# Decay attention with a routed second attention: fixed key/query tiles with 64 extra rows, weights loaded later, and products of zeros on TensorE in the first three pairs

## The chip, the cores and the metric

The kernel runs on one core of one Trainium2 chip. The metric is the device time of one execution in microseconds (us). Lower is better.

## The reference, cut to what matters

```python
# q, k, v: (8, 8, 576, 64) f32; f: (8, 8, 576) in 0.8..1.0
scores = 0.125 * q @ k.T
cum = np.cumsum(np.log(np.clip(f, 1e-4, 1.0)), axis=-1)
scores = where(causal, -1e9, scores + cum[..., :, None] - cum[..., None, :])
x = softmax(scores) @ v                      # then heads side by side: (8, 576, 512)
logits = x @ w_gate                          # 4 experts, the best 2 kept per token
for e in range(4):                           # wq, wk, wv: (4, 512, 64); wo: (4, 64, 512)
    s = 0.125 * (x @ wq[e]) @ (x @ wk[e]).T  # causal
    out += gate[..., e:e+1] * (softmax(s) @ (x @ wv[e]) @ wo[e])
```

## The kernel before, in words

Work goes in *pairs*: two heads (or two experts) of one batch. Of each of the 8 batches there are 4 attention pairs (`a0` to `a3`) and 2 expert pairs (`m0`, `m1`), 48 in all. A pair passes through these stages.

- `prep_attn` (L202): keys and queries come in natural order (`kn`, `qn`), TensorE transposes them (L221), ScalarE copies the result, rounded, into the tile `kq` (L229) and VectorE writes the rest of the rounding into the tile `ka` (L230). Two transfers inside SBUF copy the rounded half into `ka` too (L199). `prep_moe` does the same for expert pairs by products with the weights.
- `extra_rows` (L187): rows 64 to 68 of `kq` carry the decay. On the key and the query side they hold a cumulated logarithm in two parts, and ones or minus ones against it, so that one product gives score plus decay. For the first two pairs (`DIRECT = 2`) they are written by POOL memsets (L189, L190) and by two transfers from the tile `chl` (L191, L192). For all later pairs one transfer brings 5 rows from the DRAM buffer `ex` (L194). Row 68 takes the row maximum.
- `max_pass` (L369): products of `kq` with itself over 68 rows (L378), each reduced by VectorE to row maxima (L384, L395). TensorE turns the maxima (L433), ScalarE negates them (`ms`, L435), and two transfers put them into row 68 of `kq` (L199).
- `scores` (L454): the products of `ka` (L464) and of `kq` over 69 rows (L465), exponentials on ScalarE (L481 to L512), causal masks and partial row sums on POOL. `attend` (L537) multiplies by the values (`oa`, `ob`, L551).

`decay_rows` (L117) makes `chl` for all heads at the start, laid out as 32 rows of two heads, and fills `ex` with the ones, the minus ones and `chl` (L139 to L144). `load_weights` (L150) loads, splits and rounds wv, wk, wq and wo in 8 pieces of up to 576 columns: transfers (L164 to L174), a ScalarE copy (L175), a POOL subtraction (L176).

Each stage is a generator. A table gives it a start and an end on a scale on which one pair is 1.0 (`PLAN`, `HEAD` for the first 9 pairs, `TAIL` for the last), and a heap emits the pieces in that order. The weights have `l0=-1.0` to `l1=0.2` in the table `W`. A scheduler then sets the final order on each engine by priority and its own timeline. All transfers are issued by one queue, SP, in order. Each engine also runs its list in order.

```python
    def extra_rows(kq, x):
        if x < DIRECT:
            nc.gpsimd.memset(kq[64:69].bitcast(F32), 1.0)
...
        nc.sync.dma_start(
            kq[64:69].bitcast(F32), ex[x].rearrange("k r h s -> r h k s")
        )
```

Of the kernel before, what the change touches and what calls it, by code (L numbers as in the profile page):

```python
# [23 lines left out]

@with_exitstack
def tile_decay_attention_moe(ctx: ExitStack, tc, q, k, v, f, w_gate, wq, wk, wv, wo, out):
# [83 lines left out]
    ft, lf = (fl[:NP, i, : 2 * S] for i in range(2))  # L112
    nc.sync.dma_start(ft, f.rearrange("b (p h) s -> (b p) (h s)", h=2))
    chl = pair.tile([128, 2, 2, S], F32R, tag="kq", name="chl")[:NX]
    nc.gpsimd.memset(chl[NP:].bitcast(F32), 0.0)
# [654 lines left out]
```

## Time and profile before

| | |
|---|---|
| runs of the kernel | 794.36, 796.29, 798.07 us (median 796.29) |
| the profiled execution | 794.9 us, its span 793.2 us |
| mean granted TensorE clock | 0.994 |
| busy over the span: TensorE / weight load | 93% / 76% |
| busy: VectorE / ScalarE / POOL | 73% / 60% / 51% |
| DMA | 73.32 MB, mean 92 GB/s |
| chain that ended last | TensorE 74%, VectorE 8%, ScalarE 6%, DMA 5% |

In 40 equal slices of the span TensorE is busy 3, 6, 9, 8 tenths in the first four, 9 in nearly all others, and 8, 9, 9, 8, 7 in the last five. The DMA engines are busy 7, 8, 6, 5 tenths in the first four slices and about 3 later. The first 53.4 us are called the head below: they end with the last product of the first pair's `ob`.

### The profile page before, as it was taken

The page shows a single profiled execution, that of the slowest core. Times are in us where ns is not written, and L with a number is a line of the kernel's source. Part 1 is how long each engine was busy: PE and PEld are TensorE (multiplying, and loading weights), DVE is VectorE, ACT ScalarE, POOL GpSimd, SP SyncE. Part 2 cuts the span into 40 slices and gives each one's busy share as a digit, 9 for nine tenths or more (in the row PEclk, how much of TensorE's full clock was granted, in tenths as well). Part 3 has the DMA queues.
Part 4 walks back from the last instruction along what each step waited for, and adds up shares of the span by engine and source line. Part 5 has one row for each costly group of instructions (what it writes and reads, how often), then busy time and mean ns, then how long its engine had stood idle before and what let it go on. Part 6 is the DMA issues. An engine that isn't in the chain of part 4 may idle for free.

```text
span 793.2 us, 16781 instructions
## 1 busy us (share of the span) xinstructions
PE 740.0 (93%) x5704; PEld 600.7 (76%) x5704; DVE 581.6 (73%) x1858; ACT 472.8 (60%) x1152; POOL 400.8 (51%) x763
## 2 busy tenths in 40 slices
PE   3698999998999999999999999999999999989987
PEld 2475678776897788877887778878887768869854
DVE  7557786898777797787777787778777877764633
ACT  5465664575657674676556665667655755555443
POOL 7556472556446564547444644465544564473270
PEclk9998999999999999999999999999999999999999
DMA  7865541254424632355323542256323442203103
GB/s 187 194 138 118 98 105 32 58 123 89 91 51 105 145 86 49 84 128 139 79 63 87 127 107 63 52 135 147 78 65 79 112 102 57 55 21 70 58 14 106
DMA packets 143231, 73.32 MB, mean 92 GB/s; under 512 B 124085, under 2 KB 124565, under 8 KB 143081
## 3 DMA queue, kind: packets, MB, share of 16 engines
q1 hardware_dynamic: 143147, 72.26, 39.9%
q8 instruction: 45, 0.74, 0.4%
q14 instruction: 39, 0.32, 0.1%
HBM read 32.68 MB, written 10.96 MB: 55 GB/s over the span
## 4 chain that ended last, share of the span: by engine, by line
PE 74%; DVE 8%; ACT 6%; DMA 5%; SPq 3%; issue 2%; POOL 2%; POOLq 0%; ACTq 0%; DVEq 0%
PE pp_m L352 13%; PE ob_a L551 9%; PE pv L276 6%; PE po L678 6%; PE s_a L464 6%; PE s_a L465 6%; PE m_a L378 5%; PE tp_a L221 3%; PE ob_m L551 3%; PE m_m L378 3%; PE s_m L464 3%; PE s_m L465 3%; PE oa_a L551 2%; DVE junk_a L384 2%; PE sm_a L594 2%
## 5 line engine op out<-in xcount | busy, mean ns | idle before, releaser
L230 DVE TENSOR_TENSOR ka_a<-tp_a,kq_a 64x288 fp32r<-64x288 f32 x256 | 113.0, 451 | 25.0 <-ACT kq_a L229 19.4
L384 DVE CUSTOM_DVE_ANT_0 junk_a<-m_a,mask 128x192 bf16<-128x192 f32 (+2 forms) x192 | 93.3, 486 | 48.2 <-PE m_a L378 28.6
L464 PE MATMUL s_a<-ka_a 128*128 128x320 f32 (+4 forms) x384 | 115.8, 319 | 1.7 <-ACT P_a L481 1.1
L378 PE MATMUL m_a<-kq_a 68*128 68x320 f32 (+4 forms) x384 | 103.5, 337 | 14.0 <-DMA kq_a<-chl 7.8
L229 ACT ACTIVATE kq_a<-tp_a 64x288 fp32r<-64x288 f32 x256 | 99.1, 403 | 28.7 <-DVE ka_a L230 18.8
L465 PE MATMUL s_a<-kq_a 69*128 69x320 f32 (+4 forms) x384 | 104.8, 302 | 3.1 <-DMA kq_a<-ms_a 3.1
L450 POOL TENSOR_SCALAR_AFFINE_SELECT P_a<-P_a 128x128 f32<-128x128 f32 x128 | 37.5, 295 | 107.5 <-ACT P_a L496 96.1
L483 POOL TENSOR_SCALAR_AFFINE_SELECT P_a<-P_a 128x256 f32<-128x256 f32 x64 | 26.1, 408 | 125.8 <-ACT P_a L481 124.1
L378 PEld LDWEIGHTS m_a<-kq_a 68*128 68x128 f32 (+1 forms) x384 | 65.5, 191 | 26.4 <-issue 9.1
L359 ACT ACTIVATE kq_m<-pp_m 64x288 fp32r<-64x288 f32 x128 | 51.5, 405 | 51.4 <-PE pp_m L352 29.9
L360 DVE TENSOR_TENSOR ka_m<-pp_m,kq_m 64x288 fp32r<-64x288 f32 x128 | 57.8, 454 | 31.6 <-ACT kq_m L359 27.0
L464 PEld LDWEIGHTS s_a<-ka_a 128*128 128x128 f32 (+1 forms) x384 | 71.1, 186 | 8.8 <-ACT P_a L496 2.2
L519 POOL TENSOR_TENSOR R_a<-P_a 128x448 f32<-128x448 f32 x64 | 73.2, 1144 | 4.1
L551 PE MATMUL ob_a<-P_a,va 128*64 128x320 f32 (+1 forms) x512 | 73.8, 433 | 0.9 <-ACT ms_m L435 0.4
L465 PEld LDWEIGHTS s_a<-kq_a 69*128 69x128 f32 (+1 forms) x384 | 70.1, 186 | 5.7 <-DMA kq_a<-ms_a 4.3
L551 PEld LDWEIGHTS ob_a<-P_a,va 128*64 128x64 f32 x512 | 36.0, 144 | 33.4 <-issue 8.0
L464 PE MATMUL s_m<-ka_m 128*128 128x192 f32 (+3 forms) x192 | 57.9, 316 | 1.9 <-ACT P_m L496 1.2
L384 DVE CUSTOM_DVE_ANT_0 junk_m<-m_m,mask 128x192 bf16<-128x192 f32 (+2 forms) x96 | 46.6, 485 | 17.7 <-PE m_m L378 14.1
L520 POOL TENSOR_TENSOR R_a<-R_a,P_a 128x320 f32<-128x320 f32 x64 | 55.9, 875 | 1.1
L465 PE MATMUL s_m<-kq_m 69*128 69x192 f32 (+2 forms) x192 | 52.5, 300 | 3.3 <-DMA kq_m<-ms_m 3.2
L378 PE MATMUL m_m<-kq_m 68*128 68x192 f32 (+2 forms) x192 | 48.0, 317 | 0.6 <-DVE mxt_m L395 0.3
L276 PE MATMUL pv<-vh,xh_a 128*128 128x260 f32 x160 | 47.1, 294 | 1.1 <-DVE ka_a L230 1.0
(189 smaller groups left out, 2071.8 us busy)
## 6 DMA issues: line engine op xcount, KB each, us to landing
ka_a<-kq_a SPq DMA_DIRECT2D x64, 288.0 KB
kn_a<-in_k_dram SPq DMA_DIRECT2D x64, 144.0 KB
qn_a<-in_q_dram SPq DMA_DIRECT2D x64, 144.0 KB
ka_m<-kq_m SPq DMA_DIRECT2D x32, 288.0 KB
va<-in_v_dram SPq DMA_DIRECT2D x64, 128.0 KB
out_dram<-outb SPq DMA_DIRECT2D x32, 256.0 KB
kq_a<-ex SPq DMA_DIRECT2D x30, 45.0 KB
kq_a<-ms_a SPq DMA_DIRECT2D x64, 2.5 KB
```

The lines of the kernel that those rows point to most:

```text
L229: nc.scalar.activation(hv, src, AF.Copy)
L230: nc.vector.tensor_tensor(lo[:, h, gs], src, hv.bitcast(F32), ALU.subtract)
L276: nc.tensor.matmul(pv[:, :NV], l[c][:, t0 : t0 + 128], r[:, c], start=(n == 0), stop=(n == 3 * KC - 1))
L352: nc.tensor.matmul(pp[:, :HS], w[:, c, es], x[c][:, gs], start=(n == 0), stop=(n == 3 * KC - 1))
L360: nc.vector.tensor_tensor(lo[:, h, gs], src, hv.bitcast(F32), ALU.subtract)
L378: nc.tensor.matmul(dst, qB[0:K, h, i0 : i0 + dst.shape[0]], kB[0:K, h, j0:j1], start=True, stop=True)
L384: nc.vector.tensor_tensor_reduce(jk[:, :n], src, mask[:, MW - n :], 1.0, init, ALU.add, ALU.max, acc)
L464: nc.tensor.matmul(dst, kaf[:, c : c + m], qA[:, h, i0:i1], start=True, stop=False)
L465: nc.tensor.matmul(dst, kqf[0:K, c + h * S : c + h * S + m], qB[0:K, h, i0:i1], start=False, stop=True)
L519: g.tensor_tensor(r[:, h, 128:S], q[:, 320:768], q[:, 768:1216], ALU.add)
L520: g.tensor_tensor(r[:, h, 256:S], r[:, h, 256:S], q[:, 1216:1536], ALU.add)
L551: mm = nc.tensor.matmul(dst[64 * h : 64 * h + 64, c0 : c0 + rhs.shape[-1]], vs[h][0:kp, blk], rhs, start=first, stop=last,)
```

## The change

- **Key/query tiles.** `kq` no longer comes from a pool of three buffers that holds `chl` too. Four fixed tiles `kq0` to `kq3` are taken in turn. Rows 64 to 127 of each are set once (`constant_rows`: ones on the key side, zeros on the query side, minus ones in query rows 64 and 65), the first tile partly by VectorE, the rest by POOL. `max_pass` and `scores` now multiply over all 128 rows (`K = 128`). The natural tiles get four buffers in place of three.
- **Decay rows.** `decay_rows` works on 64 rows of one head each. `ex` holds only the two parts of the logarithm, in one transfer (L180), and zeros for the expert pairs. Per pair two transfers (L242, L243) of 2 rows each replace the one of 5 rows. Only the first pair takes its rows from `chl` (`DIRECT = 1`).
- **Weights.** They are due from 1.0 to 4.0 on the plan's scale, in 9 pieces: two experts in one transfer (L217).
- **Products of zeros.** `warm` multiplies a tile of zeros, 128 x 128 by 128 x 512 in BF16, into a PSUM tile that nobody reads: 8 at the start, and one behind each ScalarE copy of the first three pairs, 24 in all, each waiting for that copy.
- `PLAN`, `HEAD` and `TAIL` are moved and keep their numbers. `dynamic_dma_scratch_size=1024` frees SBUF. The asserts emit nothing.

```diff
+WARM = (1, 1, 1)
+WARM0 = 8
+W = dict(d1=-1.9, l0=1.0, l1=4.0, c0=-1.7, c1=-1.3, x0=-0.9)
...
-    nat = ctx.enter_context(tc.tile_pool(name="nat", bufs=3))
+    nat = ctx.enter_context(tc.tile_pool(name="nat", bufs=4))
...
+    NKQ = 4
+    kqs = [const.tile([128, 2, 2, S], F32R, name=f"kq{i}") for i in range(NKQ)]
+    wz = const.tile([128, 512], BF16, name="wz")
+    nc.vector.memset(wz, 0.0)
+    wps = ptile(ps_o, "o", "warm")
+    def warm(n, after=None):
+        for _ in range(n):
+            mm = nc.tensor.matmul(wps, wz[:, 0:128], wz, start=True, stop=True)
+            if after is not None:
+                together(mm, after)
+    def constant_rows(kq, eng):
+        eng.memset(kq[64:128, :, 0].bitcast(F32), 1.0)
+        nc.gpsimd.memset(kq[64:128, :, 1].bitcast(F32), 0.0)
+        nc.gpsimd.memset(kq[64:66, :, 1].bitcast(F32), -1.0)
+    constant_rows(kqs[0], nc.vector)
...
-    DIRECT = 2
-    ex = dram.tile([NX, 2, 5, 2, S], F32, name="ex")
+    DIRECT = 1
+    ex = dram.tile([NP + 1, 2, 2, S], F32, name="ex")
...
-        for kq, r0, r1, src in ((0, 2, 5, pos1), (1, 0, 2, neg1), (1, 4, 5, pos1)):
-            nc.sync.dma_start(
-                ex[:, kq, r0:r1].rearrange("x r h s -> x (r h) s"),
-                src.unsqueeze(1).to_broadcast([NX, 2 * (r1 - r0), S]),
-            )
-        nc.sync.dma_start(ex[:, 0, 0:2], chl.bitcast(F32))
-        nc.sync.dma_start(ex[:, 1, 2:4], chl.bitcast(F32))
+    def spread_rows():
+        nc.sync.dma_start(ex[:NP].rearrange("x h r s -> (x h) r s"), chl.bitcast(F32))
+        nc.sync.dma_start(
+            ex[NP].rearrange("h r s -> (h r s)").rearrange("(p c) -> p c", p=128), zero
+        )
...
+                for e in range(0, E, 2):
+                    parts.append(
+                        (w[e : e + 2].rearrange("e (c p) d -> p (e c) d", p=128), 2, slice(D * e, D * e + 2 * D))
+                    )
+                if nm == "v":
+                    parts.append((w_gate.rearrange("(c p) e -> p c e", p=128), 1, slice(E * D, NV)))
...
-        nc.sync.dma_start(
-            kq[64:69].bitcast(F32), ex[x].rearrange("k r h s -> r h k s")
-        )
+        src = ex[x].rearrange("h r s -> r h s")
+        nc.sync.dma_start(kq[64:66, :, 0].bitcast(F32), src)
+        nc.sync.dma_start(kq[66:68, :, 1].bitcast(F32), src)
...
-                    nc.scalar.activation(hv, src, AF.Copy)
+                    made = nc.scalar.activation(hv, src, AF.Copy)
                     nc.vector.tensor_tensor(lo[:, h, gs], src, hv.bitcast(F32), ALU.subtract)
+                    if u["first"] is not None:
+                        warm(WARM[u["first"]], made)
...
-        kB, qB, K = u["kB"], u["qB"], 68
+        kB, qB, K = u["kB"], u["qB"], 128
...
-        qA, qB, K = u["qA"], u["qB"], 69
+        qA, qB, K = u["qA"], u["qB"], 128
...
-    W = dict(d1=-0.8, l0=-1.0, l1=0.2)
...
-    task(-1.99, W["d1"], 1.0, decay_rows)
+    task(-1.999, W["d1"], 1.0, decay_rows)
+    task(W["c0"], W["c1"], 1.0, constants)
+    task(W["x0"], W["x0"], 1.0, spread_rows)
     task(W["l0"], W["l1"], 4.0, load_weights)
```

What it does to the order is shown at three places. First SP, from the second half of the second pair's copies to the row maxima (`ms`) of the first pair, before:

```order
L169 DMA st_q_353<-in_moe_wq_dram 128x4x64 [waits DMAHW1_49]
L169 DMA st_q_353<-in_moe_wq_dram 128x4x64 [waits DMAHW2_49]
L199 DMA ka_a_1_254<-kq_a_1_255 64x2x576 [waits DMAHW3_49,Activation_49]
L191 DMA kq_a_1_255<-chl 2x2x576 [waits DMAHW4_49,Pool_49]
L192 DMA kq_a_1_255<-chl 2x2x576 [waits DMAHW5_49]
L164 DMA st_o_365<-in_moe_wo_dram 128x512 [waits DMAHW6_49,Pool_49]
L211 DMA kn_a_2_389<-in_k_dram 96x6x64 [waits DMAHW7_49,PE_49]
L211 DMA kn_a_2_389<-in_k_dram 96x6x64 [waits DMAHW0_49]
L211 DMA qn_a_2_390<-in_q_dram 96x6x64 [waits DMAHW1_49,PE_49]
L211 DMA qn_a_2_390<-in_q_dram 96x6x64 [waits DMAHW2_49]
L199 DMA kq_a_0_163<-ms_a_0_305 1x5x128 [waits DMAHW3_49,Activation_49]
L199 DMA kq_a_0_163<-ms_a_0_305 1x5x128 [waits DMAHW4_49]
```

and now:

```order
L259 DMA qn_a_3_512<-in_q_dram 96x6x64 [waits DMAHW0_49]
L299 DMA va_104<-in_v_dram 128x4x64 [waits DMAHW1_49]
L299 DMA va_104<-in_v_dram 128x4x64 [waits DMAHW2_49]
L304 DMA va_104<-in_v_dram 64x2x64 [waits DMAHW3_49]
L299 DMA va_105<-in_v_dram 128x4x64 [waits DMAHW4_49]
L246 DMA ka_a_2_372<-kq_113 64x2x576 [waits DMAHW5_49,Activation_49]
L299 DMA va_105<-in_v_dram 128x4x64 [waits DMAHW6_49]
L304 DMA va_105<-in_v_dram 64x2x64 [waits DMAHW7_49]
L246 DMA kq_111<-ms_a_0_316 1x5x128 [waits DMAHW0_49,Activation_49]
L246 DMA kq_111<-ms_a_0_316 1x5x128 [waits DMAHW1_49,PE_49]
L217 DMA st_v_619<-in_moe_wv_dram 128x8x64 [waits DMAHW2_49]
L217 DMA st_v_672<-in_moe_w_gate_dram 128x4x4 [waits DMAHW3_49]
```

Ahead of the row maxima the weights are gone but for one piece of wv, and the loads of the fourth pair and of the first values stand there now.

Second ScalarE, from the row maxima of the first pair (`ms_a_0`) to its first exponentials (`P_a_0`), before:

```order
L435 ACTIVATE ms_a_0_305<-mp_a_0_303 10x128 [waits PE_49]
L175 ACTIVATE qh<-st_q_340 128x512 [waits DMAHW7_49,DMAHW0_49]
L175 ACTIVATE qh<-st_q_353 128x512 [waits DMAHW2_49,DMAHW1_49]
L175 ACTIVATE oh<-st_o_365 128x512 [waits DMAHW6_49]
L229 ACTIVATE kq_a_2_388<-tp_a_2_395 64x288 [waits DMAHW4_49,PE_49,DMAHW5_49,Activation_49,Pool_49]
L229 ACTIVATE kq_a_2_388<-tp_a_2_444 64x288 [waits PE_49]
L229 ACTIVATE kq_a_2_388<-tp_a_2_395 64x288 [waits DVE_49]
L175 ACTIVATE oh<-st_o_409 128x512 [waits DMAHW5_49]
L229 ACTIVATE kq_a_2_388<-tp_a_2_444 64x288 [waits DVE_49]
L481 ACT_TABLE_LOAD
L481 ACTIVATE P_a_0_369<-s_a_0_371 128x512 [waits PE_49]
```

and now:

```order
L489 ACTIVATE ms_a_0_316<-mp_a_0_314 10x128 [waits PE_49]
L277 ACTIVATE kq_114<-tp_a_3_629 64x288 [waits PE_49]
L538 ACT_TABLE_LOAD [waits PE_49]
L538 ACTIVATE P_a_0_354<-s_a_0_356 128x512 [waits Activation_49]
L220 ACTIVATE vh<-st_v_619 128x4x128 [waits DMAHW2_49]
L220 ACTIVATE vh<-st_v_672 128x4x4 [waits DMAHW3_49]
L538 ACTIVATE P_a_0_354<-s_a_0_406 128x512 [waits PE_49]
```

No weight stands between the row maxima and the first exponentials any more. Four pieces stand among the exponentials of the first pair and the rest behind them.

Third TensorE, in the second pair's maximum pass (`m_a_1`), before:

```order
L378 MATMUL m_a_1_381<-kq_a_1_255 128x192
L378 MATMUL m_a_1_381<-kq_a_1_255 128x320
L378 MATMUL m_a_1_403<-kq_a_1_255 128x192
L378 MATMUL m_a_1_403<-kq_a_1_255 128x320
L378 MATMUL m_a_1_413<-kq_a_1_255 128x256
L378 MATMUL m_a_1_420<-kq_a_1_255 128x448
L221 MATMUL tp_a_2_395<-ident,kn_a_2_389 128x96 x3
L221 MATMUL tp_a_2_444<-ident,kn_a_2_389 128x96 x3
L378 MATMUL m_a_1_413<-kq_a_1_255 128x256
L221 MATMUL tp_a_2_474<-ident,qn_a_2_390 128x96 x2
L465 MATMUL s_a_0_371<-kq_a_0_163 128x192
```

and now:

```order
L432 MATMUL m_a_1_395<-kq_112 128x256 [waits DVE_49]
L432 MATMUL m_a_1_402<-kq_112 128x448 [waits DVE_49]
L432 MATMUL m_a_1_395<-kq_112 128x256 [waits DVE_49]
L432 MATMUL m_a_1_413<-kq_112 128x448 [waits DVE_49]
L432 MATMUL m_a_1_417<-kq_112 128x320 [waits DVE_49]
L432 MATMUL m_a_1_417<-kq_112 66x64 x2
L432 MATMUL m_a_1_436<-kq_112 128x320 [waits DVE_49]
L519 MATMUL s_a_0_356<-kq_111 128x192 [waits DMAHW0_49]
```

The first scores that need the row maxima (`s_a_0<-kq`) stood inside the second pair's maximum pass, and stand behind all of it now. The 24 later products of zeros all stand ahead of the second pair's maximum pass.

## Rows read from the trace of the kernel before

**Rows 1.** Busy us of PE, PEld, DVE, ACT, POOL; clock; DMA share; GB/s.

```profile
0.00:53.40 53.40, 31.55 (x131) 23.26 (x131) 32.31 (x88) 26.48 (x57) 32.38 (x61) 1.00 0.79 179
31.20:53.40 22.20, 20.60 (x92) 15.94 (x92) 13.31 (x42) 12.04 (x28) 10.73 (x18) 1.00 0.78 167
53.40:107.00 53.60, 48.00 (x339) 33.94 (x339) 41.85 (x128) 32.60 (x82) 31.12 (x60) 0.90 0.51 105
200.00:740.00 540.00, 526.76 (x4208) 438.10 (x4210) 408.35 (x1332) 333.35 (x819) 273.42 (x523) 1.00 0.38 87
```

**Rows 2.** Timeline of TensorE, head: start us, length us, instruction [idle before <-releaser].

```profile
18.93 1.30 PE L378 MATMUL m_a<-kq_a 68*128 68x192 f32 x4 [3.04 <-DMA kq_a<-chl]
31.19 1.30 PE L378 MATMUL m_a<-kq_a 68*128 68x192 f32 x4 [4.72 <-DMA kq_a<-chl]
35.53 0.51 PE L465 MATMUL s_a<-kq_a 69*128 69x192 f32 x1
49.88 3.44 PE L551 MATMUL ob_a<-P_a,va 128*64 128x320 f32 x16
```

**Rows 3.** Timeline of TensorE: the same two shapes early and late.

```profile
46.25 0.47 PE L465 MATMUL s_a<-kq_a 69*128 69x320 f32 x1
57.44 0.31 PE L465 MATMUL s_a<-kq_a 69*128 69x320 f32 x1
47.04 1.55 PE L551 MATMUL oa_a<-P_a,va 128*64 128x256 f32 x8
59.53 0.87 PE L551 MATMUL oa_a<-P_a,va 128*64 128x256 f32 x8
```

**Rows 4.** Timeline of SP's queue, head.

```profile
3.38 2.02 SPq L139 DMA_DIRECT2D ex<-one  x3
24.54 2.31 SPq L169 DMA_DIRECT2D st_q<-in_moe_wq_dram  x4
32.06 1.55 SPq L199 DMA_DIRECT2D kq_a<-ms_a  x2
```

**Rows 5.** Timeline of ScalarE, head.

```profile
37.18 0.63 ACT L175 ACTIVATE oh<-st_o 128x512 fp32r<-128x512 f32 x1 [0.92 <-DMA st_o<-in_moe_wo_dram]
38.12 1.28 ACT L481 ACT_TABLE_LOAD   x1
39.42 1.08 ACT L481 ACTIVATE P_a<-s_a 128x512 f32<-128x512 f32 x2
47.48 0.26 ACT L512 ACTIVATE pl<-s_a 64x128 f32<-64x128 f32 x1
```

**Rows 6.** Timeline of VectorE, head.

```profile
16.36 1.38 DVE L230 TENSOR_TENSOR ka_a<-tp_a,kq_a 64x288 fp32r<-64x288 f32 x3 [0.23 <-ACT kq_a L229]
19.78 0.36 DVE L384 CUSTOM_DVE_ANT_0 junk_a<-m_a,mask 128x192 bf16<-128x192 f32 x1 [2.04 <-PE m_a L378]
25.66 0.28 DVE L428 TENSOR_REDUCE mxs_a<-mx_a 64x2 f32<-64x128 f32 x1
```

**Rows 7.** Group by line, ScalarE, 18 to 40 us: busy us, mean ns.

```profile
L175 ACT ACTIVATE kh<-st_k 128x512 fp32r<-128x512 f32 x2 | 1.3, 631 | 3.1 <-DMA st_k<-in_moe_wk_dram 3.1
```

**Rows 8.** Groups by line, POOL, 0 to 60 us.

```profile
L176 POOL TENSOR_TENSOR kl<-st_k,kh 128x512 fp32r<-128x512 f32 x2 | 2.5, 1261 | 1.2 <-DMA st_q<-in_moe_wq_dram 1.0
L190 POOL MEMSET kq_a<- 2x1152 f32 x2 | 2.1, 1054 | 0.1
```

**Rows 9.** Waits, 107 to 740 us: us in total, times, longest us.

```profile
PEld s_m L465 <- DMA kq_m<-ms_m: 4.7, 6, 1.4
PEld s_a L465 <- DMA kq_a<-ms_a: 4.3, 5, 1.3
PE s_m L465 <- DMA kq_m<-ms_m: 3.2, 4, 1.1
PE s_a L465 <- DMA kq_a<-ms_a: 3.1, 5, 1.1
```

**Rows 10.** Tile kq_a, 107 to 740 us: duration ns min/median/max.

```profile
L194 SPq DMA_DIRECT2D kq_a<-ex x24: 742/768/904, 153.0 to 648.3; - x24
```

More of the change, by code (lines that the diff above doesn't have):

```diff
@@ L106, in tile_decay_attention_moe @@
     NP = B * NPH
-    NX = NP + 1
-    DIRECT = 2
-    ex = dram.tile([NX, 2, 5, 2, S], F32, name="ex")
+    DIRECT = 1
+    ex = dram.tile([NP + 1, 2, 2, S], F32, name="ex")
+    NR = B * H
     fl = prob.tile([128, 2, 1536], F32, tag="P", name="fl")
[L112 to L115, printed above, removed]
@@ new lines, in tile_decay_attention_moe @@
+    ft, lf = (fl[:NR, i, :S] for i in range(2))
+    nc.sync.dma_start(ft, f.rearrange("b h s -> (b h) s"))
+    chl = rows.tile([128, 2, S], F32R, tag="R", name="chl")[:NR]
+    pos1 = rows.tile([128, 2, S], F32, tag="R", name="one")[:NR, 0]
+    nc.vector.memset(pos1, 1.0)
+    zero = const.tile([128, 4 * S // 128], F32, name="zero")
+    nc.vector.memset(zero, 0.0)
+    warm(WARM0)
+    def decay_rows():
+        cum = prob.tile([128, 2, 1536], F32, tag="P", name="cum")[:NR, 0, :S]
+        nc.scalar.activation(lf[:, 0:1], pos1[:, 0:1], AF.Ln)
+        nc.vector.tensor_scalar(ft, ft, 1.0e-4, 1.0, ALU.max, ALU.min)
+        nc.scalar.activation(lf, ft, AF.Ln)
+        nc.vector.tensor_tensor_scan(cum, pos1, lf, 0.0, ALU.mult, ALU.add)
+        nc.scalar.activation(chl[:, 0], cum, AF.Copy, scale=INV_SCALE)
+        nc.vector.scalar_tensor_tensor(
+            chl[:, 1], cum, INV_SCALE, chl[:, 0].bitcast(F32), ALU.mult, ALU.subtract
+        )
+        yield 1.0
@@ new lines, in load_weights @@
+            for i, (src, ne, at) in enumerate(parts):
+                st = xs.tile([128, S], F32, tag="xh", name=f"st_{nm}{i}")
+                if ne is None:
+                    nc.sync.dma_start(st[:, :DM], src)
+                    sv = st[:, :DM]
+                    h, l = hi[:, at[0]], lo[:, at[0]]
+                else:
+                    k = ne * n * (at.stop - at.start) // ne
+                    nc.sync.dma_start(st[:, :k].rearrange("p (x d) -> p x d", x=ne * n), src)
+                    sv = st[:, :k].rearrange("p (e c d) -> p c e d", e=ne, c=n)
+                    h, l = (t[:, :, at].rearrange("p c (e d) -> p c e d", e=ne) for t in (hi, lo))
+                nc.scalar.activation(h, sv, AF.Copy)
+                nc.gpsimd.tensor_tensor(l, sv, h.bitcast(F32), ALU.subtract)
+                yield 4.0 / 9
@@ L185, in new_pair @@
+    def new_pair(u, nm):
+        ka = pair.tile([128, 2, 2, S], F32R, tag="ka", name="ka" + nm)
+        i = n_pair[0] % NKQ
+        n_pair[0] += 1
+        assert kq_user[i] is None or kq_user[i].get("scored")
+        kq_user[i] = u
+        kq = kqs[i]
         return ka, ka[:, 0], ka[:, 1], kq, kq[:, :, 0], kq[:, :, 1]
@@ L261, in moe_front @@
             vm = [v_att[0], v_att[1]]
+            assert all(u is None or u.get("attended") for u in v_user[:2]) and natt[0] == B * NPH
         else:
@@ L710, in tile_decay_attention_moe @@
     for i, (kind, b, p) in enumerate(seq):
-        u = dict(kind=kind, b=b, p=p)
+        u = dict(kind=kind, b=b, p=p, first=i if i < len(WARM) else None)
         t = pos[i]
```

164 lines of the change are left out of this document (70 added, 94 removed).

## The prediction, as put on record

> **What bounds the kernel now.** I read the busy times by stretch first, to see where TensorE is not at work, then the timelines of the head, engine by engine, and last the waits of the long middle. From 200 to 740 us TensorE is busy 526.8 of 540 us [rows 1]: there TensorE is the bound, and a head that ends earlier moves everything behind it forward by as much. In the head, the first 53.4 us, TensorE is busy 31.6 us and the DMA engines carry 179 GB/s at a share of 0.79, against 0.38 later [rows 1]. What to see there are three things.
>
> Transfers come late. The first pair's maximum pass starts at 18.93 us and had waited for the decay rows (`kq_a<-chl`); the second pair's starts at 31.19, after 4.72 us of waiting for the same kind of rows [rows 2]. SP issues one transfer behind the other, among them ones and minus ones for `ex` at 3.38 us and weights at 24.54, and comes to the row maxima only at 32.06 [rows 4].
>
> ScalarE then waits for weights. It runs in order, and a piece of wo at 37.18 us that had waited for its transfer, and a table load at 38.12, stand ahead of the first exponentials, which run at 39.42 [rows 5]. The scores they read had begun at 35.53 [rows 2].
>
> TensorE is slow. The granted clock reads 1.00 in the head [rows 1], but the same product of 320 columns takes 0.47 us at 46.25 and 0.31 at 57.44, and the eight of `oa` take 1.55 us and then 0.87 [rows 3]. So before some 53 us it runs at the lower of its two levels, 1.2 GHz, and behind it at 2.4. By the column of the clock alone, products of zeros have nothing to gain, and only the sum below is left (787.5); by the durations, a case of 782 stands beside it (the first rival). The Trainium skill (TensorE: Matmul & The Clock Gate, Part 1) says that the half rate is the default and that activity lifts it, and warns that clock events in a trace can't be fully trusted. The durations agree with it.
>
> **The change part by part.** The sum goes along the first pair, up to the end of its `ob`, which is at 49.88 + 3.44 us and four small products, about 53.4 [rows 2].
>
> *Transfers ahead of the first decay rows.* By their shapes, f, four loads of keys and four of queries, the ones (33 x 12 x 576 x 4 bytes, 912 KB), `chl` into `ex` twice (608 KB), a piece of wv and half a copy make 3.27 MB before. Now it is f, the same eight loads, two for the third pair, a larger piece of wv and the half copy: 2.19 MB. The difference at 179 GB/s [rows 1] is 6.1 us, so the rows should land at about 13 us in place of 18.9.
>
> *VectorE is late next.* Before, the last splits of the second pair end at 16.36 + 1.38 = 17.7 us [rows 6]. The work on the logarithms halves, since 64 rows go at once, and memsets of about 1.4 us come in, so I put this 1 to 2 us earlier, and the maximum pass of the first pair, which now stands ahead of the last of these splits, at 15.5. The pass takes 19.78 to 25.94, 6.2 us [rows 6], and stands mixed with 9 splits of 0.46 us (three take 1.38 [rows 6]), so it ends at about 26. That is no gain. But the second pair's pass follows at once, because its rows are there, and ends at about 32, where before it began at 31.19 [rows 2] and ended far behind the first scores.
>
> *The scores.* They now stand behind that pass, and begin at about 32 in place of 35.53. This loses part of what the earlier rows give. `ms` has until then: about 37 transfers stand ahead of it, at about 0.7 us each (two for 1.55 [rows 4]) some 26 us, so it is issued at about 27 and hidden by the second pass.
>
> *The exponentials.* No weight stands ahead; one us of products and the table load of 1.28 us [rows 5] do. They start at about 34.2 in place of 39.42: 5.2 us gained. From there to the end of the last exponential (`pl`, 47.74 [rows 5]) it was 8.3 us; that stretch holds 4.3 us of exponentials and copies and now 2.4 us of weights and small pieces, 6.7 in all: 1.6 us gained. Behind it TensorE has `oa`, `ob`, transposes and the end of the third pair's pass, 6.3 us at the low clock, against 5.7 before: 0.6 us lost. The end of `ob` comes at about 47.2, **6.2 us earlier**.
>
> *What is done by then.* The third pair's maximum pass is done, of which before two thirds, 4 us on VectorE, were still to come; fewer splits of the fourth pair are done. The next stretch has TensorE busy 48.0 and VectorE 41.9 of 53.6 us [rows 1], so work ahead is worth something but not its full length: between 0 and 4 us, I take **2**, nearer the one us that TensorE needs for it.
>
> *The weights* leave the head. A piece costs ScalarE 0.63 us [rows 7] and POOL 1.26 us [rows 8]. Five of nine come behind the first exponentials, 3 us on ScalarE and 6 on POOL, where these are busy 32.6 and 31.1 of 53.6 us [rows 1]. That idle time hides them, and without this cover it would be up to 3 us on the path. I take **0.3** lost.
>
> *The products of zeros.* No row shows one. By the 0.31 and 0.47 us for 320 columns [rows 3], 512 columns take at most 0.50 or 0.75 us. The 24 behind copies take 12 to 18 us on TensorE, which in the first 31.2 us is busy only 31.6 - 20.6 = 11 us [rows 1]: they fit in its idle time. But each waits for a ScalarE copy, and transposes and maximum products queue behind it. The bounds are 0 and, one behind every second of fourteen products, 4 us; VectorE is the slower one there and has two PSUM tiles to read, so I take **0.4** lost. For the clock I take nothing in the sum: the last of them stands ahead of the second pair's pass, and that pass is limited by VectorE, so TensorE has little to do from about 26 to 32 us and I expect it at the low level when the scores begin.
>
> *Constant rows.* Eleven memsets of 1152 elements on POOL at 1.05 us [rows 8], 11.6 us, replace about 8 us of memsets; POOL has nothing else early. Products over 128 rows in place of 68 or 69: `ka` with 128 rows and `kq` with 69 take turns in the chain, and the time goes by columns; at nothing, with no bound beyond 0.
>
> *The long middle.* Of `ex`, 94 transfers of two rows replace 46 of five (two for 47 pairs, one for 46), each at about 0.77 us of SP [rows 10], and bytes fall from 45 to 18 KB a pair. SP is idle in between, so nothing; the bounds are in the rivals. A fourth buffer for `nat` may give a us. The scheduler shuffles the order everywhere, plus or minus 2 us.
>
> Sum: 6.2 + 2 - 0.3 - 0.4 = **7.5 us** off the profiled 794.9: 787.4, called 787.5. The median of the runs shown is 796.29, 1.4 above that execution, so a like median could be 789. A measurement of this kernel tells about 0.5%, 4 us, from no change: faster means under 792.3.
>
> **The rivals.**
>
> *The clock stays up.* If the zeros lift TensorE to 2.4 GHz and it holds through the first scores, `oa` and `ob` lose 0.7 and 1.3 us ([rows 3], and `ob` in proportion), the products ahead of the exponentials about 1.5: 784. From 53.4 to 107 the mean clock is 0.90 [rows 1], which is about 5 us lost; if the earlier state also keeps some of this, 779 to 784, I say 782. For it: TensorE at the low level is busy 20.6 of 22.2 us just before 53.4 [rows 1], so there it does set the pace. Against: the idle stretch of the second pass.
>
> *The gain is given back.* The weights meet value loads and natural tiles at 40 to 80 us, where DMA carries 105 GB/s already [rows 1]; ScalarE stops in order behind each late piece, and the exponentials with it. Two stops like the 0.9 us at 37.18 [rows 5] for each of four pairs, 7 us: no change, 792.5 to 797.
>
> *More transfers, slower.* Place: SP, just ahead of the row maxima of a pair. In the middle the first scores wait for them 4.7 + 4.3 + 3.2 + 3.1 = 15.3 us in 20 waits [rows 9]. If the extra issue of 0.77 us [rows 10] falls between `ms` being ready and its issue, the wait grows by it. With 10 such pairs of 47 the gain is gone; with all 20 that wait now and the 4 us on both sides of a late landing it is 15 us lost: 802. Against it: one transfer of 45 KB becomes two of 9 KB, and an issue stands directly ahead of `ms` in only few pairs. The Trainium skill (DMA: Bandwidth & Descriptors, Bandwidth) says that transfers under 64 KB are dominated by their descriptors and should be merged, which speaks against the split; no row here shows the smaller size.
>
> **How the numbers follow.** Forecast (low clock, 787.5, from 783.5 to 791.5 by the bounds of the terms): 0.50. The clock stays up (782): 0.26. Given back (792.5 to 797): 0.16. More transfers (802): 0.08. The first two are faster: 0.76; same 0.16; slower 0.08. The range goes from 779, the low end of the second, to 794.5, the middle of the third, and leaves out 0.08 above it by the last, about 0.08 of the third, and a little below.
>
> **What would show it.** Right: the first pair's maximum pass at 15 to 16 us, the second's directly behind, first exponentials near 34, the end of `ob` near 47, and products of 320 columns at 0.47 us between 32 and 45. If those take 0.31, it is the second case. Wrong: a head that ends at 50 or later, pauses of ScalarE before weights from 35 to 70 us, or longer waits for `ms` in the middle than 15 us.

## The result, and the profile after

The changed kernel takes 787.2 us in the median (785.06 to 788.92, 6 runs) against 795.3 (792.63 to 798.61, 6 runs) for the kernel before on the same chip. The ratio is 0.9896, with an interval from 0.9862 to 0.9929: **faster by about 1%**. The profiled execution takes 786.67 us with a span of 785.0.

TensorE bounds the middle, so I read first where its span goes: busy or idle. Busy times by engine, from the page of the kernel before:

```profile
span 793.2 us, 16781 instructions
PE 740.0 (93%) x5704; PEld 600.7 (76%) x5704; DVE 581.6 (73%) x1858; ACT 472.8 (60%) x1152; POOL 400.8 (51%) x763
```

The same part of the page after:

```profile
span 785.0 us, 16899 instructions
PE 740.4 (94%) x5735; PEld 594.7 (76%) x5736; DVE 584.9 (75%) x1857; ACT 469.5 (60%) x1151; POOL 404.0 (51%) x770
```

The products of zeros alone, of the changed kernel, 0 to 60 us (busy us of PE; clock; DMA share; GB/s):

```profile
0.00:60.00 60.00, 13.07 (x31) 0.86 0.91 173
```

Before, TensorE is idle for 793.2 - 740.0 = 53.2 us, after for 785.0 - 740.4 = 44.6. Its busy time is the same only by chance: 13.1 us of it are zeros (the trace has 31 of the 32), so the real products take 727.3 us, 12.7 less than before. So the 8.2 us are 8.6 us less idle time; 12.7 us of faster products were paid back by 13.1 us of zeros.

Busy times by stretch, after (columns as in [rows 1]):

```profile
0.00:53.40 53.40, 43.35 (x220) 28.13 (x222) 38.63 (x115) 29.71 (x71) 35.01 (x74) 0.84 0.93 174
31.20:53.40 22.20, 19.72 (x122) 14.69 (x123) 14.72 (x54) 15.51 (x38) 16.85 (x29) 0.91 0.92 170
53.40:107.00 53.60, 46.30 (x337) 35.05 (x338) 46.96 (x120) 34.67 (x83) 33.36 (x60) 0.94 0.51 111
200.00:740.00 540.00, 525.67 (x4217) 434.71 (x4216) 410.23 (x1335) 329.97 (x816) 272.71 (x520) 1.00 0.36 85
```

From 200 to 740 us nothing has changed against [rows 1]. In the head VectorE does 38.6 us of work where it did 32.3, and from 53.4 to 107 it is busy 47.0 us in place of 41.9. The timeline of TensorE, head, after:

```profile
16.04 0.50 PE L432 MATMUL m_a<-kq 128*128 128x192 f32 x2
...
27.37 1.30 PE L432 MATMUL m_a<-kq 128*128 128x192 f32 x4
...
33.29 0.36 PE L519 MATMUL s_a<-kq 128*128 128x192 f32 x1
...
34.52 0.47 PE L519 MATMUL s_a<-kq 128*128 128x320 f32 x1
...
39.19 0.30 PE L519 MATMUL s_a<-kq 128*128 128x320 f32 x1
...
42.96 0.87 PE L600 MATMUL oa_a<-P_a,va 128*64 128x256 f32 x8
...
44.76 2.16 PE L600 MATMUL ob_a<-P_a,va 128*64 128x320 f32 x16
...
46.75 0.28 PE L600 MATMUL ob_a<-pl,va 128*64 128x64 f32 x4
```

The first pass begins at 16.04 us, the second follows at 27.37 without the wait of 4.72 us of [rows 2], and the first `ob` ends at 47.03 in place of 53.4. The 320 columns take 0.47 us at 34.52 and 0.30 at 39.19, so the clock rises in the middle of the first pair's scores and not at 53 us [rows 3]. VectorE between the two passes:

```profile
26.65 0.28 DVE L482 TENSOR_REDUCE mxs_a<-mx_a 64x2 f32<-64x128 f32 x1
28.23 0.36 DVE L438 CUSTOM_DVE_ANT_0 junk_a<-m_a,mask 128x192 bf16<-128x192 f32 x1 [1.30 <-PE m_a L432]
...
34.12 0.28 DVE L482 TENSOR_REDUCE mxs_a<-mx_a 64x2 f32<-64x128 f32 x1
```

ScalarE at the first exponentials:

```profile
34.32 1.28 ACT L538 ACT_TABLE_LOAD   x1 [4.73 <-PE s_a L519]
35.61 0.60 ACT L538 ACTIVATE P_a<-s_a 128x512 f32<-128x512 f32 x1
36.11 0.72 ACT L220 ACTIVATE vh<-st_v 128x512 fp32r<-128x512 f32 x2
...
41.33 0.26 ACT L569 ACTIVATE pl<-s_a 64x128 f32<-64x128 f32 x1
```

No weight stands ahead of them now, and the weights behind them (`vh`) had landed in time: none of the waits of ScalarE from 35 to 70 us is for a weight. The transfers of SP that matter:

```profile
9.10 0.80 SPq L238 DMA_DIRECT2D kq<-chl  x1
...
30.11 1.65 SPq L246 DMA_DIRECT2D kq<-ms_a  x2
```

The waits for row maxima from 107 to 740 us, which were 15.3 us in 20 waits [rows 9], are 11.9 in 22:

```profile
PEld s_m L519 <- DMA kq<-ms_m: 5.4, 10, 0.9
...
PEld s_a L519 <- DMA kq<-ms_a: 3.4, 5, 1.2
PE s_m L519 <- DMA kq<-ms_m: 3.1, 7, 0.7
```

The lead of 6.4 us at the first `ob` grows to 15.7 at the fourth (94.0 before, 78.3 after), falls to 5.4 at the ninth (170.5 and 165.1), and is 8.1 at the last. TensorE's clock has a part in these swings. Behind the head it falls to 0.50 twice more in either kernel, each time behind a stretch in which TensorE had paused: before from about 73 to 80 and from 90 to 93.5 us, after from 97 to 103 and from 161.5 to 165, some 10 us in each. In the changed kernel, around the first of these falls, and from the first `ob` to the ninth (busy us of PE; clock; DMA share; GB/s):

```profile
93.50:96.50 3.00, 1.29 (x11) 1.00 0.97 205
97.00:103.00 6.00, 5.93 (x26) 0.50 0.03 6
47.03:165.10 118.07, 107.73 (x840) 0.96 0.43 95
```

### The profile page after: what moved, and what is told of

It reads as the page before. It is cut to its first block, busy times and chain, and to the rows that moved or that the text cites. A ratio compares the mean times of both kernels' runs of the same rounds, so it can differ in the third digit from the quotient of the medians.

```text
span 785.0 us, 16899 instructions
## 1 busy us (share of the span) xinstructions
PE 740.4 (94%) x5735; PEld 594.7 (76%) x5736; DVE 584.9 (75%) x1857; ACT 469.5 (60%) x1151; POOL 404.0 (51%) x770
## 4 chain that ended last, share of the span: by engine, by line
PE 74%; DVE 10%; ACT 6%; DMA 5%; issue 2%; SPq 2%; POOL 1%; POOLq 0%; DVEq 0%; ACTq 0%
PE pp_m L406 13%; PE ob_a L600 8%; PE pv L330 7%; PE po L727 7%; PE s_a L518 6%; PE m_a L432 6%; PE s_a L519 5%; PE tp_a L269 4%; PE s_m L519 3%; PE m_m L432 3%; PE s_m L518 3%; DMA kq<-ms_m 3%; PE sm_a L643 2%; DVE ka_a L278 2%; DMA kq<-ms_a 2%
## 5 line engine op out<-in xcount | busy, mean ns | idle before, releaser
L278 DVE TENSOR_TENSOR ka_a<-tp_a,kq 64x288 fp32r<-64x288 f32 x256 | 113.3, 451 | 18.8 <-ACT kq L277 8.5
L277 ACT ACTIVATE kq<-tp_a 64x288 fp32r<-64x288 f32 x256 | 100.2, 403 | 36.7 <-DVE ka_a L278 25.3
L438 DVE CUSTOM_DVE_ANT_0 junk_a<-m_a,mask 128x192 bf16<-128x192 f32 (+2 forms) x192 | 93.5, 487 | 37.0 <-PE m_a L432 29.8
L518 PE MATMUL s_a<-ka_a 128*128 128x320 f32 (+4 forms) x384 | 113.1, 314 | 2.6 <-ACT P_a L538 1.8
L432 PE MATMUL m_a<-kq 128*128 128x320 f32 (+4 forms) x384 | 102.0, 328 | 7.3 <-DVE mxs_a L438 5.5
L519 PE MATMUL s_a<-kq 128*128 128x320 f32 (+4 forms) x384 | 100.6, 297 | 2.2 <-DMA kq<-ms_a 2.2
L414 DVE TENSOR_TENSOR ka_m<-pp_m,kq 64x288 fp32r<-64x288 f32 x128 | 58.2, 454 | 44.8 <-ACT kq L413 42.7
L413 ACT ACTIVATE kq<-pp_m 64x288 fp32r<-64x288 f32 x128 | 51.8, 404 | 62.4 <-PE pp_m L406 40.3
L432 PEld LDWEIGHTS m_a<-kq 128*128 128x128 f32 (+1 forms) x384 | 63.8, 185 | 21.1 <-DVE mxs_a L438 11.8
L519 PEld LDWEIGHTS s_a<-kq 128*128 128x128 f32 (+1 forms) x384 | 68.8, 184 | 4.9 <-DMA kq<-ms_a 3.4
L519 PE MATMUL s_m<-kq 128*128 128x192 f32 (+2 forms) x192 | 50.6, 297 | 3.2 <-DMA kq<-ms_m 3.1
L432 PE MATMUL m_m<-kq 128*128 128x192 f32 (+2 forms) x192 | 48.4, 318 | 1.2 <-ACT ms_m L489 0.5
```

Source lines behind the costliest of these rows:

```text
L277: made = nc.scalar.activation(hv, src, AF.Copy)
L278: nc.vector.tensor_tensor(lo[:, h, gs], src, hv.bitcast(F32), ALU.subtract)
L414: nc.vector.tensor_tensor(lo[:, h, gs], src, hv.bitcast(F32), ALU.subtract)
L432: nc.tensor.matmul(dst, qB[0:K, h, i0 : i0 + dst.shape[0]], kB[0:K, h, j0:j1], start=True, stop=True)
L438: nc.vector.tensor_tensor_reduce(jk[:, :n], src, mask[:, MW - n :], 1.0, init, ALU.add, ALU.max, acc)
L518: nc.tensor.matmul(dst, kaf[:, c : c + m], qA[:, h, i0:i1], start=True, stop=False)
```

## The experiments

Each line of the table is one kernel: its median, its ratio to the kernel before on the same chip, and from its one profiled execution the span, TensorE's busy time, the zeros' part of it, and the idle time (span less busy). Executions of one kernel scatter over 2.5 to 10 us, so a median of 4 to 6 runs tells 4 us, hardly 2. The idle and busy times are of single executions. Those of zeros_first_only, no_zeros_68_69, weights_early and no_zeros_nat3 are 2.2 to 3.8 us faster than the median of their kernel, so their spans flatter them.

Much of the scatter goes with the granted clock. Of 44 executions of the kernel before, the eleven with a mean clock of 0.998 have spans of 790.8 to 792.8 us, and the five with 0.987 or 0.989 have 795.9 to 799.8. A change of a few us can therefore be a change in how often the clock falls.

| kernel | us | ratio [interval] | span | busy | zeros | idle |
|---|---|---|---|---|---|---|
| before | 795.0 to 796.6 | 1 | 793.2 | 740.0 | 0 | 53.2 |
| changed | 787.2 | 0.9896 [0.9862, 0.9929] | 785.0 | 740.4 | 13.1 | 44.6 |
| after_again (the same) | 784.9 | 0.9855 [0.9828, 0.9882] | 784.1 | 740.2 | 13.3 | 43.9 |
| no_zeros | 783.0 | 0.9855 [0.9828, 0.9883] | 781.2 | 734.6 | 0 | 46.6 |
| no_zeros_again | 783.2 | 0.9837 [0.9809, 0.9865] | 781.7 | 734.4 | 0 | 47.3 |
| zeros_first_only | 786.2 | 0.9871 [0.9822, 0.9920] | 782.0 | 737.7 | 3.5 | 44.3 |
| rows_68_69 | 786.2 | 0.9895 [0.9865, 0.9926] | 783.7 | 747.3 | 13.5 | 36.4 |
| no_zeros_68_69 | 786.8 | 0.9867 [0.9820, 0.9914] | 781.4 | 737.1 | 0 | 44.3 |
| weights_early | 787.0 | 0.9895 [0.9860, 0.9931] | 782.7 | 738.2 | 13.5 | 44.5 |
| ones_traffic | 786.5 | 0.9872 [0.9829, 0.9914] | 785.2 | 734.2 | 0 | 51.0 |
| no_zeros_nat3 | 781.2 | 0.9800 [0.9775, 0.9826] | 777.1 | 732.2 | 0 | 44.9 |
| before_weights_late | 798.0 | 1.0039 [1.0004, 1.0074] | 797.1 | 746.4 | 0 | 50.7 |
| ones_late_in_before | 798.9 | 1.0035 [1.0009, 1.0061] | 795.8 | 740.0 | 0 | 55.8 |
| before_nat4 | 800.1 | 1.0042 [1.0019, 1.0064] | 799.7 | 743.7 | 0 | 56.0 |

### The zeros

```diff
-WARM = (1, 1, 1)
-WARM0 = 8
+WARM = (0, 0, 0)
+WARM0 = 0
```

> The changed kernel without its 32 products of zeros, all else as it is. Theory (earlier transfers and weights out of the way give the gain, zeros next to nothing): within 2 us of the changed kernel, 785 to 789, the first ob ends at 46 to 48 us, and the lift to 2.4 GHz still comes at about 36 us, since the products at 33 to 36 us have nothing to do with zeros. Rival (the zeros give the gain by the clock): low level until the first ob, which ends at 50 us or later; 790 to 793.

Measured 783.0 us. Timeline of TensorE without zeros, products of 320 columns:

```profile
34.67 0.47 PE L519 MATMUL s_a<-kq 128*128 128x320 f32 x1
...
41.45 0.46 PE L519 MATMUL s_a<-kq 128*128 128x320 f32 x1
...
48.85 0.31 PE L519 MATMUL s_a<-kq 128*128 128x320 f32 x1
```

The clock rises some 6 us later than with zeros, the real products take 734.6 us in place of 727.3, and still the span is 3.8 us shorter. Zeros buy 7.3 us of faster products and 2.0 us of idle time for 13.1 us of their own. The first pass begins at 14.47 us in place of 16.04. Both kernels were run again side by side, five rounds each:

> The changed kernel once more, on the same chip as the other three of this call, to set the cost of the zeros against the scatter of the runs. Theory (zeros cost): 3 to 5 us more than the kernel without zeros, beside it on the same chip. Rival (the difference of the earlier call was scatter): within 1.5 us of it.

> The changed kernel without zeros once more, beside the changed kernel on the same chip. Theory (zeros cost): 0.984 to 0.987 of the kernel before, 3 to 5 us less than the changed kernel. Rival (scatter): 0.988 to 0.991 of the kernel before, as the changed kernel.

The difference of the medians is 1.7 us here, where it was 4.2 at first, and 2.4 us of the spans. That is between the two expectations. Medians and spans agree in sign both times and give **1.7 to 4.2 us** for the zeros, but the intervals of the ratios overlap. Which of the zeros cost:

```diff
-WARM = (1, 1, 1)
+WARM = (0, 0, 0)
 WARM0 = 8
```

> The changed kernel with its first eight products of zeros, and without the 24 between the transposes. Theory (each of the 24 waits for a ScalarE copy, and transposes and maximum products queue behind it): the first maximum product comes near 14.5 us in place of 16.0, as without any zeros, and the time is 782 to 784.5. Rival (zeros of either place cost, or the difference lies in the order of later work): 785.5 to 788, as the changed kernel.

By its median, 786.2, this is the rival's number; by the trace it is the theory: the first pass begins at 14.27 us and every `ob` up to the ninth ends 0.2 to 0.6 us behind the kernel without zeros (163.6 and 163.0 at the ninth), with a span of 782.0. But that execution is the fastest of its four. The runs reach from 783.97 to 787.48, so the time leaves it open.

### The rows and the clock

```diff
-        kB, qB, K = u["kB"], u["qB"], 128
+        kB, qB, K = u["kB"], u["qB"], 68
...
-        qA, qB, K = u["qA"], u["qB"], 128
+        qA, qB, K = u["qA"], u["qB"], 69
```

> The changed kernel with the products of the maximum pass over 68 rows and those of the scores over 69, as before; the constant rows are still set. Theory (the time of a product goes by columns, and the clock does not care about rows): 785 to 789, lift at about 36 us, first ob ends at 47. Rival (128 rows in place of 68 or 69 are what lifted the clock at 35.6 us, where 22 us of nearly unbroken products at the low level did not before): low level up to the first ob, which ends at 50 us or later; 790 to 793.

Busy time and granted clock of TensorE with 68 and 69 rows, zeros as in the change (busy us of PE; clock; DMA share; GB/s):

```profile
24.00:36.00 12.00, 10.66 (x35) 0.50 0.71 152
36.00:42.00 6.00, 5.33 (x17) 0.50 1.31 205
42.00:50.00 8.00, 8.00 (x37) 0.50 0.81 143
50.00:60.00 10.00, 9.77 (x71) 0.95 0.54 122
```

The same stretches of the changed kernel:

```profile
24.00:36.00 12.00, 10.18 (x35) 0.57 0.74 160
36.00:42.00 6.00, 4.77 (x24) 1.00 1.34 207
42.00:50.00 8.00, 7.47 (x62) 1.00 0.90 178
50.00:60.00 10.00, 9.92 (x73) 1.00 0.75 161
```

With the wider products the clock rises earlier: with 128 rows it is at 2.4 GHz from 36 us on, with 68 and 69 it stays at 1.2 GHz until about 50, though TensorE is busy 8.00 of 8.00 us from 42 to 50 (in part with products over 128 rows, those of `ka`, `oa` and `ob`). The first `ob` ends at 51.1 us in place of 47.0. And yet the total is the same: by the ninth pair's `ob` (162.8 us against 165.1) the loss is gone. The table shows how: 6.5 us more of real products (733.8 and 727.3), 8.2 less idle. One thing more differs. Behind the first `ob` the clock of this kernel does not fall again up to the ninth, as it does in the changed one, and the stretch between the two is 6.4 us shorter:

```profile
51.10:162.84 111.74, 105.57 (x849) 1.00 0.43 94
```

The edit also moved the order of the program: the products come in the order of the changed kernel only up to 28 us. So it is not shown that the slow clock of the head costs nothing; it may cost, and another order may have saved the later falls.

The same without zeros:

> The changed kernel without any zeros and with products over 68 and 69 rows. Theory (neither the clock nor the end of the first ob decides the total): products of 320 columns take 0.47 us up to about 50 us (without zeros but with 128 rows the shorter 0.31 came at about 42), the first ob ends at 50 to 52, and still the time is 782 to 785. Rival (with the zeros gone, the clock of the head counts in full): 3 to 4 us more than without zeros alone, 786 to 788.

The trace gives the theory's picture (320 columns at 0.47 us up to 42.4, at 0.31 from 52 on; first `ob` at 51.1; span 781.4 against 781.2). The median, 786.8, is the rival's, but its runs reach from 783.08 to 788.5, and the ratios of the two kernels overlap. The profiled execution is the fastest of the four and the only one with a mean clock of 1.000; the others have spans of 784.8 to 786.8 us at 0.988 to 0.993. So a cost of the slow clock of up to 4 us isn't excluded. For the rise itself this pair is the cleaner one: up to 41 us both kernels run their products in the same order, and just behind, the eight products of `oa` take 0.87 us (at 42.34) with 128 rows and 1.55 with 68 and 69:

```profile
43.49 1.55 PE L600 MATMUL oa_a<-P_a,va 128*64 128x256 f32 x8
```

### The weights

```diff
-W = dict(d1=-1.9, l0=1.0, l1=4.0, c0=-1.7, c1=-1.3, x0=-0.9)
+W = dict(d1=-1.9, l0=-1.0, l1=0.2, c0=-1.7, c1=-1.3, x0=-0.9)
```

> The changed kernel with the weights due from -1.0 to 0.2 as before, still in 9 larger pieces. Theory (about half of the gain is that no weight stands ahead of the first exponentials): the first exponentials at 38 us or later in place of 35.6, first ob ends at 50 or later, 790 to 793. Rival (the removed ones and the doubled logarithm work carry the gain, weights were hidden): first exponentials within 1.5 us of 35.6 and 786 to 789.

ScalarE with the weights early again:

```profile
39.59 1.28 ACT L538 ACT_TABLE_LOAD   x1 [1.10 <-PE s_a L519]
40.89 1.09 ACT L538 ACTIVATE P_a<-s_a 128x512 f32<-128x512 f32 x2
```

The first exponentials come 5.3 us later and the first `ob` ends 3.9 us later, at 50.9. The total doesn't move: 787.0 against 787.2, and by the ninth pair (164.0) it is ahead; its clock is at 0.50 for 3.4 us behind the first `ob`, not for 10. The other way round, in the kernel before:

```diff
-    W = dict(d1=-0.8, l0=-1.0, l1=0.2)
+    W = dict(d1=-0.8, l0=1.0, l1=4.0)
```

> The kernel before with the weights due from 1.0 to 4.0 and nothing else changed. Theory: decay rows still land late, but the row maxima are issued at once and no weight stands ahead of the exponentials: first exponentials at about 35 us in place of 39.4, first ob at about 50 in place of 53.4, 790 to 793. Rival (later weights alone do nothing, or collide with values and natural tiles later): 794 to 798.

It is slower by 0.4% (1.0039, with an interval that begins at 1.0004). But the edit didn't do what it was meant to do. ScalarE:

```profile
41.16 0.63 ACT L175 ACTIVATE kh<-st_k 128x512 fp32r<-128x512 f32 x1 [1.21 <-DMA st_k<-in_moe_wk_dram]
43.11 1.09 ACT L481 ACTIVATE P_a<-s_a 128x512 f32<-128x512 f32 x2
```

The first exponentials come at 43.11 us, later than the 39.42 of [rows 5] and not at 35. The row maxima are issued at 35.99 in place of 32.06 [rows 4], and a weight that had waited for its transfer still stands ahead of the exponentials. The first `ob` ends 4.7 us later (58.2), the ninth 2.5 earlier (168.0). The time is lost behind it, where the clock is at 0.50 for some 14 us (near 612, 645 and 763 us) and in the kernel before not at all. So the run says nothing about weights that are out of the way. With weights_early it shows that the first pair's exponentials aren't what the end hangs on.

### The transfers ahead of the first rows

To the kernel without zeros I gave back the bytes that the change removes, into a buffer that nothing reads:

```diff
+        for r0, r1 in ((0, 3), (3, 5), (5, 6)):
+            nc.sync.dma_start(dummy[:, r0:r1], pos1.unsqueeze(1).to_broadcast([NR, r1 - r0, S]))
...
+        nc.sync.dma_start(dummy[:, 6:8], chl.bitcast(F32))
```

> The kernel without zeros, plus transfers that nothing reads: 64 rows of ones, six times 576 elements (885 KB, as three transfers right behind the first pair's keys and queries, where the kernel before had them), and the decay rows once more (295 KB) ahead of the first pair's rows. Theory (the removed transfers carry the gain, since the first decay rows land earlier and VectorE, which is 95% busy from 60 to 100 us, gets its maximum passes done earlier): 1.18 MB at 179 GB/s are 6.6 us, so the first maximum product comes at 19 to 21 us where it came at 14.5 without zeros, VectorE is idle 4 to 6 us longer up to the ninth pair's ob, and the time is 787 to 790. Rival (the order, the logarithms of 64 rows at once, or the fourth buffer carry it): the first maximum product may come later, but the time stays within 2 us of the 783.0 without zeros.

Busy times from its page, and its first maximum product:

```profile
span 785.2 us, 16847 instructions
PE 734.2 (94%) x5704; PEld 594.1 (76%) x5704; DVE 583.7 (74%) x1857; ACT 472.1 (60%) x1151; POOL 405.7 (52%) x770
```

```profile
15.46 0.82 PE L436 MATMUL m_a<-kq 128*128 128x192 f32 x2
```

The busy time stays and the idle time grows by 4.4 us. The first product comes only 1 us later than without the traffic (I had expected 5), but from the first `ob` (3.4 us later) to the ninth (3.2) and to the end (span 4.0 longer) the delay is carried along whole. The clock behind the head is the same in both (at 0.50 for some 7 us). That is the one edit of the study whose cost goes straight through. The median is 3.5 us above that without zeros, just under the range of the theory and outside that of the rival; the two ratios come from different chips and overlap, so the size rests on the spans, 4.0 us.

Moving the same transfers behind the first weights in the kernel before does not give this back:

```diff
+    task(-0.5, -0.5, 1.0, spread_rows)
```

(`spread_rows` holds the five transfers into `ex`, taken out of `decay_rows`.)

> The kernel before, with the five transfers into ex (ones, minus ones, decay rows) issued behind the first weights instead of ahead of the first pair's rows; all else as before. Theory (transfers ahead of the first rows): the first maximum product comes at 14 to 16 us where it came at 18.9; the second pair's rows still stand behind its last splits and come near 27, so only a part is gained: 789 to 793. Rival (the first pair's rows don't matter, what comes later sets the time): 794 to 797, as the kernel before.

Timeline of TensorE:

```profile
15.46 1.31 PE L384 MATMUL m_a<-kq_a 68*128 68x192 f32 x4
...
33.95 1.30 PE L384 MATMUL m_a<-kq_a 68*128 68x192 f32 x4 [8.33 <-DMA kq_a<-chl]
```

The first pair's pass comes 3.5 us earlier, as expected, but the bytes now stand ahead of the second pair's rows: TensorE waits 8.33 us for them in place of 4.72 [rows 2]. Idle time is 2.6 us longer and the kernel slower. The wait was moved, not removed.

### The fourth natural buffer

In the kernel without zeros:

```diff
-    nat = ctx.enter_context(tc.tile_pool(name="nat", bufs=4))
+    nat = ctx.enter_context(tc.tile_pool(name="nat", bufs=3))
```

> The changed kernel without zeros and with three buffers for the natural tiles, as the kernel before has, in place of four. Theory (the fourth buffer carries most of what the removed transfers don't, since a pair's keys and queries are loaded and split further ahead): the ninth pair's ob ends 3 to 4 us later than without zeros alone, at 166 to 167 us, and the time is 3 to 6 us more than that of the kernel without zeros on this chip. Rival (the rest of the gain lies in the new order of the head and in the smaller rows of ex): the same time within 1.5 us, with the ninth pair's ob at 162 to 164.

And in the kernel before:

```diff
-    nat = ctx.enter_context(tc.tile_pool(name="nat", bufs=3))
+    nat = ctx.enter_context(tc.tile_pool(name="nat", bufs=4))
...
-num_devices=1)
+num_devices=1, dynamic_dma_scratch_size=1024)
```

> The kernel before with four buffers for the natural tiles (and the small scratch that makes room for them), all else as before. Theory (the fourth buffer): 3 to 5 us less than the kernel before, a ratio of 0.994 to 0.996, with the ninth pair's ob 3 to 4 us earlier than the 170.5 of before. Rival (buffers don't matter while transfers and VectorE fill the head): within 1.5 us of the kernel before.

Both went against the theory, and further than the 1.5 us of the rivals: with four buffers the kernel before is slower by 0.4% (1.0042, interval above 1), and with three the kernel without zeros takes 2.0 us less beside it on the same chip (the intervals just overlap; 4.6 us of the spans). Without zeros and with four buffers, busy times by stretch (columns as in [rows 1]):

```profile
60.00:100.00 40.00, 34.58 (x251) 24.11 (x250) 34.10 (x90) 24.11 (x60) 25.32 (x45) 0.91 0.54 120
100.00:200.00 100.00, 95.14 (x777) 78.17 (x776) 81.49 (x255) 63.48 (x157) 53.42 (x101) 1.00 0.34 76
```

With three:

```profile
60.00:100.00 40.00, 36.02 (x280) 26.55 (x278) 37.12 (x102) 27.55 (x67) 26.53 (x48) 1.00 0.54 120
100.00:200.00 100.00, 98.34 (x798) 79.52 (x796) 76.31 (x248) 61.11 (x154) 54.83 (x103) 1.00 0.36 80
```

At the fifth pair both are level (its `ob` ends at 96.8 and 96.4 us). Then the sixth takes 20.7 us with four buffers and 14.1 with three. Two things differ ahead of it. With three, VectorE has done 37.1 us of work from 60 to 100 us in place of 34.1. And with four the clock is at 0.50 from 83 to 90 us (the mean of 0.91), while with three it stays at 1.00. The number of buffers also reshuffles the order of the program. Which of these carries the gain was not tried. At 781.2 us, ratio 0.9800, this is **the fastest kernel of the study**: 3.7 us below the changed kernel on the same chip.

In the kernel before, what the fourth buffer costs goes with the clock. At the ninth `ob` it is 1.2 us behind (171.6 and 170.5); the rest is lost later, where the clock falls three times (near 197, 617 and 648 us). From the ninth `ob` to the end, with three buffers and with four:

```profile
170.48:793.20 622.72, 597.57 (x4719) 1.00 0.37 85
171.63:799.70 628.07, 601.69 (x4719) 0.99 0.36 84
```

At the same mean clock, 0.989, the two don't differ: nine executions with four buffers have spans of 796.4 to 800.3 us, four with three 795.9 to 799.8. Why the clock falls more often with four isn't shown.

## Why the prediction was right, and where it was not

The total was right: 787.5 forecast, 787.2 measured; of the profiled execution 7.5 us were summed and 8.2 came off. Of its steps some were right, and some wrong ones cancelled.

- **Transfers and the two passes: right in kind.** The second pass follows the first directly. I had the first at 15.5 to 26 and the second to 32; they end at 26.9 and 34.4. The row maxima are issued at 30.1 and not at 27, still ahead of the scores at 33.3. The first exponentials come at 35.6 and not at 34.2, so 3.8 us were gained there, not 5.2. The 6.1 us of transfers are worth 4 us at the end, by the run that gives the bytes back.
- **"No weight stands ahead": wrong as a cause.** In this kernel ScalarE did wait for TensorE's scores (4.73 us), and not for weights. With weights early the exponentials come 5.3 us later, and the end doesn't move. Nothing speaks against the 0.3 us for their work: no wait of ScalarE from 35 to 70 us is for a weight.
- **The end of `ob` at 47.2: hit (47.0), partly by luck.** I had the stretch from the exponentials to the end of `ob` at the low clock; it ran at the high one, and held more of the third pair's work.
- **The chain itself: the main flaw.** I summed along the first pair and let its lead run to the end. Two kernels whose first `ob` ends 4 us later have the same total. One reading of the traces is that what carries is how much of VectorE's work (splits and passes) the head gets done: in the changed kernel VectorE is busy 47.0 of the next 53.6 us and TensorE 46.3, so an earlier `ob` meets a full VectorE. The other is the clock behind the first `ob`. The stretch from there to the ninth takes 118.1 us in the changed kernel with some 10 us at 0.50, 115.6 without zeros with 7, 113.1 in weights_early with 3.4, and 111.7 to 112.0 in the three kernels whose clock doesn't fall there. The pauses ahead of the falls and the falls come together, and no run parted them. Of the sum only the "2" for work done by then points to the first reading; the second stands in no term, and in the rival only as the 5 us lost from 53.4 to 107.
- **The zeros, 0.4 us: mis-sized term.** They cost 1.7 to 4.2 us. The upper bound of 4 was about right; I took the lower end, because VectorE is slower there. But the first pass begins 1.6 us later with them (16.04 and 14.47).
- **The clock, nothing in the sum: wrong.** The low level at the first scores was right (0.47 us at 34.52), but I had it last to the end of `ob`, and it ended at 35 to 36 us. The rival "the clock stays up" was half right: the zeros lifted the clock from 14 to 24 us, it fell at 25 as they ended, and it was up again for most of the scores, `oa` and `ob`. The real products take 12.7 us less; 7.3 of these are gone without zeros. The rival's time (782) was not reached, since the zeros cost more than they gave, and since the falls behind the head, of which the rival counted some 5 us, stayed at 10 us of low clock. Without zeros the clock rises at 42 anyway, and the time is 783.
- **128 rows, "at nothing, with no bound beyond 0": not refuted by the times, wrong in kind.** The clock rises earlier with them. **The fourth buffer, "may give a us": wrong sign.** Idle time and waits of the middle stayed as they were, as forecast: `ms` waits 11.9 us in place of 15.3, so two small transfers for one large cost nothing to be seen.

So errors of opposite sign met: the zeros and the fourth buffer took some 2 to 4 us each, and the faster clock gave back more than I had counted. That the sum met the measured time within 1 us is luck. The Trainium skill (TensorE: Matmul & The Clock Gate, Part 1) says that activity lifts the half rate, and the changed trace agrees: while zeros stand between the transposes, from 14 to 24 us, the granted clock reads 0.97, and without these zeros (zeros_first_only) 0.50 in the same stretch. That the rise would come with 128 rows at 36 us, and with 68 and 69 only near 50, was not to be read from the kernel before.

What stays open: the kernel without zeros and with the traffic is still 8 us of span ahead of the kernel before, 5.8 of them busy and 2.2 idle. Faster products behind 128 rows are a part (2.5 us of busy time between the two kernels without zeros); how the rest is shared by the logarithms of 64 rows at once, the smaller `ex` and the new order was not tried one by one.

## What to carry to other kernels

An earlier first result can be worth nothing when the stretch behind the head is held by something else, here by VectorE's work or by a clock that falls after pauses: ask what brings that work forward and what keeps TensorE from pausing, and remove bytes that stand ahead of several pairs' first rows rather than move them, since a moved transfer only makes the next pair wait. Split a change of the span into busy and idle time of the bounding engine: products of zeros that lift the clock then show what they buy beside what they take. Before a difference of half a per cent is put down to an edit, compare the kernels at the same mean clock too. Where a change is a bundle, take parts out one at a time even when the sum comes out right: here, without the zeros and the fourth buffer, the bundle gains 15.1 us in place of 11.4 on the same chip.
